# Bursts of three key tiles, casts on ScalarE and a one-pass transpose in an attention and Fourier mixing kernel

## Chip, core and metric

The kernel runs on one core of one Trainium2 chip. The metric is the device time of one execution in microseconds.

## What is computed

`x` is 2048 x 640, in fp32. The output mixes an attention block and a Fourier block by a gate for each row:

```python
qkv = x @ wqkv                       # 32 heads of 20
p = softmax(q @ k.T * 20 ** -0.5)    # for each head, 2048 x 2048
a = (p @ v) @ wo
y = Cr @ (x @ Er.T) - Ci @ (x @ Ei.T)    # DFT matrices over 640 (E) and 2048 (C)
g = sigmoid((x * gate_w).sum(-1))
out = g * a + (1 - g) * y
```

## The kernel before

One loop feeds TensorE with three kinds of work, in an order that is written out by hand.

**Scores.** Heads are taken in pairs; a unit is one pair and one half of the 1024-row halves of the queries, 32 units in all, of 32 steps each. Scores are computed twice. For the maxima, a step makes two matmuls (one for each head, on the upper and the lower 64 rows of the array, 60 of them used) at L187, and VectorE reduces each 128x512 result at L189. For the exponentials, a step makes two matmuls with 62 rows at L907 (the two more rows bring in the maximum of each query) and ScalarE takes each result through Exp at L909. Maxima run 41 steps ahead (`LEAD`). A step pair (`e` or `m`) uses one half of the array for each head; the letters' heads are set by the tuples beside the order string.

**Products with v (bursts).** The exponentials p are multiplied by v in `av_step`, L528, 21 output columns for each of two heads and two query halves: four matmuls side by side in four column groups of the array, in fp32, each of two passes. In the trace a key tile is 8 instructions. They accumulate over 16 key tiles in the bank `av`, which ScalarE copies to `o` when the unit ends (`unit_end`, L536). These matmuls stand together in a burst (`burst`), at the end of each cycle of four steps: two key tiles, 16 instructions in the trace.

**Fills.** Between the scores stand pieces of other products, split into two halves of 64 rows (banks yp0 and yp1, 320 columns): first the DFT over 640 (`hid_tile`, L363, the hidden part), then that over 2048 (`dft_step`, L608, the sequence part), then the product with `wo` (`out_tile`, L715, the output part). The sequence part has 7 products of 8 units with 16 steps of 3 fills each. `fill` issues as many as the table `goals` allows up to each letter F.

**The order.** `ORDERS` holds strings: e and m are score matmuls, F a place for fills, B the burst. The hidden part has its own string for a cycle of four steps, the sequence part another, the output part a third. A sequence unit spans three cycles.

**Operands of the sequence part.** A c part (128x1024) comes from `load_c`: one or two DMAs, a sum or difference on POOL if there are two (L501), a cast to fp32r and the difference to the cast (`split`, L114 and L115), all on POOL. Each serves 8 of a unit's 16 steps. An a tile (128x320) comes from `load_a` in the same way (L512, L517, L114, L115), and `run_extras` issues one of them in each burst while the product's turn lasts. When a unit of the sequence part ends, ScalarE and VectorE read its banks (L627, L628) and POOL adds the result to y (L742, `finish_y`).

**Maxima.** When a unit's maxima are done, `max_nm` (L203) reduces them to 128x16, `max_chain` transposes them on TensorE (L221) behind the burst, VectorE splits the result into two fp32r parts (L114, L115), and SP sends four rows into the query stack (L229, L230), before the exponentials of that unit start.

**Banks.** Five PSUM banks ps0 to ps4 rotate over the scores and transposes, one is `av`, two are yp0 and yp1. Each engine runs its instructions in the order written; SP issues all DMAs of the loop in order.

Of the kernel before, what the change touches and what calls it, by code (L numbers as in the profile page):

```python
# [18 lines left out]
P = 128  # L19
# [56 lines left out]
def mix_kernel(ctx: ExitStack, tc: tile.TileContext, xa, wqk, wb, cdft, wo, out):  # L76
# [12 lines left out]
    ps_a = pools(name="ps_a", bufs=1, space=PSUM)  # L89
# [110 lines left out]

    def max_nm(n):
        nms[n] = small.tile([P, 16], F32, name="nm", bufs=2)
        dve.tensor_reduce(nms[n], mx.pop(n).rearrange("p h q c -> p (h q) c"), axis=AX.X, op=ALU.max, negate=True)  # L203
# [14 lines left out]
    def max_chain(n):  # L218
        q = q_unit(n)
        pt = bank()[:16, :P]  # L220
        pe.transpose(pt, nms.pop(n), ident)  # L221
        m1 = small.tile([16, P], R, name="m1")
        m2 = small.tile([16, P], R, name="m2")
        split(m1, m2, pt, dve, dve)

        def rows():
            for h in range(2):
                b = 64 * h + KROWS
                sp.dma_start(f32(q[b : b + 1, :]), f32(m1[8 * h : 8 * h + 8, :]))  # L229
                sp.dma_start(f32(q[b + 1 : b + 2, :]), f32(m2[8 * h : 8 * h + 8, :]))  # L230

        if now[0] < 0:
            rows()
        else:
            at_step(now[0] + 2, rows)
# [4 lines left out]
    av = ps_a.tile([P, 512], F32, name="av")  # L240
    dve.memset(av, 0.0)
# [5 lines left out]
    def load_v(n):  # L247
# [5 lines left out]
        sp.dma_start(vts[n], v_scr[p])  # L253
# [10 lines left out]
    def load_first():  # L264
        wr, w = raw_tile()[:, : ND * P].rearrange("p (d c) -> p d c", d=ND), part_tile()
        w = w.rearrange("p z c -> p (z c)")[:, : 2 * ND * P].rearrange("p (z d c) -> p z d c", z=2, d=ND)
# [11 lines left out]
        split(w[:, 0, :1], w[:, 1, :1], wr[:, :1], act, dve)  # L278
        for d in range(ND):
            if d == 1:  # L280
                split(w[:, 0, 1:], w[:, 1, 1:], wr[:, 1:], act, dve)
            split(xs[0][:, 0, d], xs[0][:, 1, d], xr[d][1], act, dve)

    def load_wqk(c):
# [3 lines left out]
        def finish():  # L288
            w = part_tile().rearrange("p z c -> p (z c)")[:, : 2 * ND * P].rearrange("p (z d c) -> p z d c", z=2, d=ND)
            split(w[:, 0], w[:, 1], raw, act, dve)  # L290
# [26 lines left out]
    def qk_tile(c, t):  # L317
        w = wt[c]
        ps = bank()
        for d in range(ND):  # L320
            three(ps, w[:, 0, d], w[:, 1, d], xs[t][:, 0, d], xs[t][:, 1, d], d == 0, d == ND - 1)
# [13 lines left out]
    def v_pair(hf, s):  # L335
        vst = v_tile().rearrange("p s e -> p (s e)").rearrange("p (a k e) -> p a k e", a=NP // 2, k=2)
# [151 lines left out]
    def load_c(g):  # L488
# [9 lines left out]
        def finish():  # L498
            c = cparts[g] = part_tile()
            if len(raws) > 1:  # L500
                pool.tensor_tensor(raws[0], raws[0], raws[1], op=ALU.add if PRODUCTS[n][0][1][0] > 0 else ALU.subtract)  # L501
            split(c[:, 0], c[:, 1], raws[0], pool, pool)

        return finish

    def load_a(n, s):
# [7 lines left out]
        def finish():  # L514
            a = a_tile(n % 2, s)
            if len(raws) > 1:
                pool.tensor_tensor(raws[0], raws[0], raws[1], op=ALU.add if PRODUCTS[n][1][1][0] > 0 else ALU.subtract)  # L517
            split(a[:, 0], a[:, 1], raws[0], pool, pool)

        return finish  # L520

    def av_step(i, n, kt):
        v = vts[n]
        pp = [pts.pop((n, kt, qc)) for qc in range(2)]
        for qc in range(2):
            for h in range(2):
                j = 2 * qc + h
                pe.matmul(av[32 * j : 32 * j + DH + 1, :], v[:, kt, h * (DH + 1) : (h + 1) * (DH + 1)],  # L528
# [4 lines left out]
    def unit_end(i, n):  # L533
        p, u = VISITS[n]
        o = pa.tile([P, 512], F32, name="o", bufs=2)
        act.activation(o, av, AF.Copy)  # L536
# [513 lines left out]
```

## Time and profile before

| | us |
|---|---|
| median of 3 runs | 1869.67 |
| lowest and highest | 1867.93, 1871.03 |
| profiled execution | 1869.47 |
| its span | 1867.7 |
| granted clock of TensorE in it | 0.998 |

The profile's page gives, for each engine, the time in which it had an instruction running; PE is TensorE's matmuls, PEld its weight loads, DVE is VectorE, ACT ScalarE, POOL GpSimd and SP the engine that issues the DMAs. The views used below are the busy times in windows of the span, the waits (who waited for whom), the groups of instructions by line and shape, and the timeline, where instructions of one line that follow each other are merged (x16) and the first two columns are start and length. The groups give busy time and the mean length of one instruction, and idle time before them.

### The profile page before, as it was taken

Reading aid. Unit: us, or ns where it says so; the run is one execution under the profiler, and the core shown is the slowest. Engines: PE = TensorE matmul, PEld = TensorE weight load, DVE = VectorE, ACT = ScalarE, POOL = GpSimd, SP = SyncE. Lnnn points to the kernel's source line nnn. Section 1 sums busy time; section 2 is a strip of 40 time slices with the busy share of each in tenths; the row PEclk is TensorE's granted clock in tenths of the full one; section 3 lists DMA queues with packets and bytes.
Section 4 is the critical chain, followed back from the end, with each engine's and each line's share of the span. In section 5 each row is a group of like instructions: output and inputs, shape, how many; then the busy total and the mean of one; then the engine's idle time right before and its main releaser. Section 6 shows DMA issues by size and latency. Waiting matters only on the chain.

```text
span 1867.7 us, 45004 instructions
## 1 busy us (share of the span) xinstructions
PE 1858.3 (100%) x17606; PEld 1360.8 (73%) x17606; DVE 1383.7 (74%) x2310; ACT 1272.1 (68%) x2439; POOL 1162.6 (62%) x1038
## 2 busy tenths in 40 slices
PE   9999999999999999999999999999999999999998
PEld 8988777676767777777777777767777777776666
DVE  3044458787878888888888888888888888888853
ACT  4222258787877777777777777777777777778885
POOL 3335432121146897466799899867779989635544
PEclk9999999999999999999999999999999999999999
DMA  6744341222134674535567576546476766431233
GB/s 230 174 136 151 139 127 56 78 65 68 54 99 139 209 209 142 161 128 175 185 192 241 163 249 191 176 140 179 145 240 203 214 198 202 142 90 47 88 98 108
DMA packets 178771, 281.61 MB, mean 151 GB/s; under 512 B 44811, under 2 KB 113547, under 8 KB 178559
## 3 DMA queue, kind: packets, MB, share of 16 engines
q1 hardware_dynamic: 177599, 276.77, 47.4%
q0 software_dynamic: 960, 1.97, 0.6%
q8 instruction: 138, 2.26, 0.5%
q14 instruction: 74, 0.61, 0.1%
HBM read 214.61 MB, written 63.52 MB: 149 GB/s over the span
## 4 chain that ended last, share of the span: by engine, by line
PE 98%; DMA 1%; POOL 0%; ACT 0%; DVE 0%; issue 0%; SPq 0%; POOLq 0%; ACTq 0%
PE av L528 25%; PE yp L608 19%; PE ps L907 16%; PE ps L187 15%; PE yp L363 7%; PE ps L118 4%; PE ps L120 4%; PE ps L119 4%; PE yp L715 3%; PE ps L221 0%; DMA p<-in_xa 0%; POOL p L115 0%; DMA a_scr<-raw 0%; DVE mx L189 0%; ACT p L323 0%
## 5 line engine op out<-in xcount | busy, mean ns | idle before, releaser
L189 DVE TENSOR_REDUCE mx<-ps 128x1 f32<-128x512 f32 x2048 | 1280.1, 684 | 298.9 <-PE ps L187 280.7
L909 ACT ACTIVATE p<-ps 128x512 f32<-128x512 f32 x2048 | 1109.1, 599 | 371.6 <-PE ps L187 248.9
L187 PE MATMUL ps<-kst,qst 60*128 60x512 f32 x1920 | 758.3, 410 | 0.0
L907 PE MATMUL ps<-qst,kst 62*128 62x512 f32 x1920 | 744.9, 407 | 0.1
L608 PE MATMUL yp<-x,part 64*128 64x320 f32 x5376 | 662.1, 306 | 0.3 <-ACT raw L373 0.3
L608 PEld LDWEIGHTS yp<-x,part 64*128 64x128 f32 x5376 | 624.7, 186 | 8.3 <-ACT raw L373 0.6
L528 PE MATMUL av<-p,v 128*21 128x512 f32 x4096 | 490.1, 596 | 0.0
L907 PEld LDWEIGHTS ps<-qst,kst 62*128 62x128 f32 x1920 | 348.1, 185 | 182.5 <-DVE mx L189 132.2
L187 PEld LDWEIGHTS ps<-kst,qst 60*128 60x128 f32 x1920 | 342.2, 184 | 7.9 <-issue 4.2
L115 POOL TENSOR_TENSOR part<-raw,part 128x1024 fp32r<-128x1024 f32 (+1 forms) x128 | 288.0, 2250 | 10.3
L528 PEld LDWEIGHTS av<-p,v 128*21 128x21 f32 x4096 | 97.6, 100 | 221.5 <-issue 218.3
L363 PE MATMUL yp<-wb,x 64*128 64x320 f32 x1920 | 224.0, 307 | 0.0
L374 POOL TENSOR_TENSOR raw<-raw 128x320 f32<-128x320 f32 x64 | 55.7, 870 | 268.4 <-ACT raw L373 219.1
L363 PEld LDWEIGHTS yp<-wb,x 64*128 64x128 f32 x1920 | 210.1, 186 | 6.0
L114 POOL CAST part<-raw 128x1024 fp32r<-128x1024 f32 (+1 forms) x128 | 126.1, 985 | 127.9 <-PE ps L187 67.0
L501 POOL TENSOR_TENSOR raw<-raw,raw 128x1024 f32<-128x1024 f32 x77 | 185.9, 2414 | 7.5 <-DMA raw<-in_cdft 6.0
L115 POOL TENSOR_TENSOR x<-araw,x 128x320 fp32r<-128x320 f32 x112 | 97.8, 873 | 9.0
L715 PE MATMUL yp<-x,part 64*128 64x320 f32 x768 | 102.2, 308 | 0.0
L323 ACT ACTIVATE p<-ps 128x512 f32<-128x512 f32 x40 | 23.8, 597 | 102.0 <-PE ps L120 85.5
L715 PEld LDWEIGHTS yp<-x,part 64*128 64x128 f32 x768 | 92.0, 186 | 1.0
L118 PE MATMUL ps<-x,part 128*128 128x512 f32 x200 | 80.7, 403 | 1.6 <-ACT x L112 1.3
L114 POOL CAST p<-p 128x512 fp32r<-128x512 f32 x40 | 24.7, 618 | 92.4 <-ACT p L323 92.4
(110 smaller groups left out, 1419.5 us busy)
## 6 DMA issues: line engine op xcount, KB each, us to landing
raw<-in_cdft SPq DMA_DIRECT2D x192, 512.0 KB
araw<-a_scr SPq DMA_DIRECT2D x192, 160.0 KB
qk_scr<-p SPq DMA_DIRECT2D x40, 512.0 KB
kst<-qk_scr SPq DMA_DIRECT2D x84, 160.0 KB
qst<-qk_scr SPq DMA_DIRECT2D x84, 160.0 KB
yt<-y_scr SPq DMA_DIRECT2D x80, 160.0 KB
a_scr<-raw SPq DMA_DIRECT2D x64, 160.0 KB
y_scr<-yt SPq DMA_DIRECT2D x64, 160.0 KB
```

Of the source, the lines that this page charges most:

```text
L114: e1.tensor_copy(dst1, src)
L115: e2.tensor_tensor(dst2, src, f32(dst1), op=ALU.subtract)
L118: pe.matmul(ps, st1, mv1, start=first, stop=False)
L187: pe.matmul(ps, q[b : b + KROWS, qt * P : (qt + 1) * P], k[b : b + KROWS, kc * 512 : (kc + 1) * 512], start=True, stop=True)
L189: return lambda: dve.tensor_reduce(mx[n][:, h, qt, kc : kc + 1], ps, axis=AX.X, op=ALU.max)
L363: pe.matmul(yp[h][:, :HE], x[r, xz, d, cs], w[r, wz, d, :HE], start=d == 0 and z == 0, stop=d == ND - 1 and z == 2)
L501: pool.tensor_tensor(raws[0], raws[0], raws[1], op=ALU.add if PRODUCTS[n][0][1][0] > 0 else ALU.subtract)
L528: pe.matmul(av[32 * j : 32 * j + DH + 1, :], v[:, kt, h * (DH + 1) : (h + 1) * (DH + 1)], pp[qc][:, h, :], start=kt == 0, stop=kt == NS - 1)
L608: pe.matmul(yp[h][:, :HE], c[r, cz, cs], a[r, az], start=s == 0 and z == 0, stop=s == NS - 1 and z == 2)
L715: pe.matmul(yp[h][:, :HE], o[oz][r], wos[d, hf][r, wz], start=d == 0 and z == 0, stop=end)
L907: pe.matmul(pt, k[b : b + KROWS + 2, kt * P : (kt + 1) * P], q[b : b + KROWS + 2, qc * 512 : (qc + 1) * 512], start=True, stop=True)
L909: act.activation(pts[n, kt, qc][:, h], pt, AF.Exp, scale=float(DH) ** -0.5)
```

## The change

The sequence part gets a string of its own with six steps a cycle, so that a unit of it spans two cycles and a burst takes three key tiles. Since 16 key tiles aren't a multiple of three, a burst may now end one unit of scores and begin the next; the accumulator then changes banks (`next_av`) within the six that scores and accumulator share, and five are left for the scores as before. v is padded so that 32 columns instead of 21 are taken for each head. The casts of c parts and of a tiles go to ScalarE within the burst (`run_preps`), while POOL makes the sum of a c part in the fill of step 2 of 8, and the sum of an a tile one burst before its cast. Loads of a tiles are spread over the product, one a burst and two in every fourth. The buffers for parts go from 3 to 2, those for p from 5 to 7. `finish_y` comes 3 instead of 5 steps after the read at the earliest. The maxima are split into two fp32r parts before the transpose, which becomes one ordinary fp32r matmul of 128 columns of weights with the identity; a copy of its first 32 rows takes the place of the split behind it. The hidden and the output part keep their strings.

```diff
 ORDERS = (
     ("ememFFFeFFmeFFmFeFmFeFmFmFFeFemB", (0, 0, 1, 0), (1, 1, 0, 1)),
+    ("ememeFFFFmeFFemFeFmFemFeFeFmeFFmeFFFFmmemmB", (0, 0, 0, 1, 0, 1), (1, 1, 0, 1, 0, 0)),
+    ("emFeFmFeFFmFeFFmeFFmeFFmFmFeFmeB", (1, 0, 1, 1), (0, 1, 0, 0)),
     ("emFFeFmFeFFmFeFmFeFFmeFmFFmFemeB", (0, 1, 1, 0), (1, 0, 0, 1)),
-    ("emFeFmFeFFmFeFFmeFFmeFFmFmFeFmeB", (1, 0, 1, 1), (0, 1, 0, 0)),
 )
...
-    turn = itertools.count()
+    places = collections.deque(f"ps{k}" for k in range(6))
...
     def bank():
-        return ps_w.tile([P, 512], F32, name=f"ps{next(turn) % 5}")
+        places.rotate(-1)
+        return place_tile(places[-1])

     def pair_tile():
-        return work.tile([P, 2, 512], F32, name="p", bufs=5)
+        return work.tile([P, 2, 512], F32, name="p", bufs=7)
...
     def part_tile():
-        return work.tile([P, 2, 1024], R, name="part", bufs=3)
+        return work.tile([P, 2, 1024], R, name="part", bufs=2)
...
     def v_tile():
-        return work.tile([P, NS, VW], F32, name="v", bufs=2)
+        return work.tile([P, NS * VW + 16], F32, name="v", bufs=2)
...
     def max_nm(n):
-        nms[n] = small.tile([P, 16], F32, name="nm", bufs=2)
-        dve.tensor_reduce(nms[n], mx.pop(n).rearrange("p h q c -> p (h q) c"), axis=AX.X, op=ALU.max, negate=True)
+        nm = small.tile([P, 16], F32, name="nm", bufs=2)
+        dve.tensor_reduce(nm, mx.pop(n).rearrange("p h q c -> p (h q) c"), axis=AX.X, op=ALU.max, negate=True)
+        nms[n] = turned
+        split(nms[n][:, :16], nms[n][:, 16:32], nm, dve, dve)
...
-        pt = bank()[:16, :P]
-        pe.transpose(pt, nms.pop(n), ident)
-        m1 = small.tile([16, P], R, name="m1")
-        m2 = small.tile([16, P], R, name="m2")
-        split(m1, m2, pt, dve, dve)
+        pt = bank()[:, :P]
+        pe.matmul(pt, nms.pop(n), ident_r, start=True, stop=True)
+        mt = small.tile([32, P], F32, name="m1")
+        dve.tensor_copy(mt, pt[:32])
...
+    def next_av():
+        places.append(av["name"])
+        av["name"] = places.popleft()
+        av["tile"] = place_tile(av["name"])
...
-        def finish():
-            c = cparts[g] = part_tile()
+        def combine():
             if len(raws) > 1:
                 pool.tensor_tensor(raws[0], raws[0], raws[1], op=ALU.add if PRODUCTS[n][0][1][0] > 0 else ALU.subtract)
-            split(c[:, 0], c[:, 1], raws[0], pool, pool)
-
-        return finish
+
+        def parts(e1):
+            c = cparts[g] = part_tile()
+            split(c[:, 0], c[:, 1], raws[0], e1, pool)
+
+        return combine, parts
...
-    def av_step(i, n, kt):
+    def av_step(i, n, kt, split_unit):
         v = vts[n]
+        if split_unit:
+            next_av()
+        t, c0 = av["tile"], kt * VW
...
-                pe.matmul(av[32 * j : 32 * j + DH + 1, :], v[:, kt, h * (DH + 1) : (h + 1) * (DH + 1)],
+                pe.matmul(t[32 * j : 32 * j + 32, :], v[:, c0 + h * (DH + 1) : c0 + h * (DH + 1) + 32],
                           pp[qc][:, h, :], start=kt == 0, stop=kt == NS - 1)
...
-        if s % 8 == 4 and cfin and g // 8 + 2 < 2 * UNITS:
-            cfin.pop(0)()
+        if s % 8 == 2 and g // 8 + 2 < 2 * UNITS:
+            cfin[0][0]()
...
-                extras.append((now[0] + 5, functools.partial(finish_y, out_, t, m, y)))
+                extras.append((now[0] + 3, functools.partial(finish_y, out_, t, m, y)))
...
+    def run_preps(c):
+        if cfin and (done - HIDS) // 24 + 1 < 2 * UNITS:
+            cfin.pop(0)[1](act)
+        while preps["combined"]:
+            preps["combined"].pop(0)[1](act)
+        while preps["loaded"]:
+            preps["combined"].append(preps["loaded"].pop(0))
+            preps["combined"][-1][0]()
+        n = c // (2 * HT) + 1
+        if n < len(PRODUCTS):
+            k = made.get(n, 0)
+            made[n] = min(NS, k + 1 + (c % 4 == 3))
+            preps["loaded"].extend(load_a(n, s) for s in range(k, made[n]))
...
     for u in range(UNITS):
-        edge.append(edge[-1] + 3)
+        edge.append(edge[-1] + 2)
...
     def burst(c):
         for n in ends:
             max_nm(n)
-        run_extras(max(done - HIDS, 0) // 3, 2)
-        for kt in (2 * c, 2 * c + 1):
-            av_step(now[0], kt // NS, kt % NS)
+        k, _, i = phase(c)
+        steps = 6 if k == 1 else 4
+        run_extras(steps - 2)
+        if k == 1:
+            run_preps(c - HID)
+        for kt in range(i // 2, (i + steps) // 2):
+            av_step(now[0], kt // NS, kt % NS, kt % NS == 0 and kt > i // 2)
         while ends:
             max_chain(ends.pop(0))
```

`load_a` is split into `combine` and `parts` in the same way as `load_c`; the first tiles and parts, in the hidden part, are still made on POOL at once (`finished`).

More of the change, by code (lines that the diff above doesn't have):

```diff
@@ L1 @@
+import collections
 import functools
@@ L807, in mix_kernel @@
             share = count * (c + 1 - c0) // (c1 - c0) - count * (c - c0) // (c1 - c0)
-            places = order_of(c)[0].count("F")
-            goals[c] = [at_goal + share * (f + 1) // places for f in range(places)]
+            fills_ = order_of(c)[0].count("F")
+            goals[c] = [at_goal + share * (f + 1) // fills_ for f in range(fills_)]
             at_goal += share
@@ L892, in score @@
         i, z = divmod(x, 2)
-        h = z ^ first[kind][(i - (LEAD if kind == "m" else 0) - 1) % 4]
+        h = z ^ first[kind][(i - (LEAD if kind == "m" else 0) - 1 - base) % len(first[kind])]
         if kind == "m":
@@ L922, in burst @@
             next_pool()
-    first = dict(zip("em", ORDERS[0][1:]))
+    base, first = 0, dict(zip("em", ORDERS[0][1:]))
     for kind in "emme":
         score(kind)
-    for c in range(total // 4):
-        first = dict(zip("em", order_of(c)[1:]))
-        for kind in order_of(c)[0]:
+    for c in range(len(goals)):
+        k, base, i = phase(c)
+        order, *heads_ = ORDERS[k]
+        first = dict(zip("em", heads_))
+        for kind in order:
             if kind == "F":
@@ L953, in take @@
             pool.tensor_tensor(y, y, m, op=ALU.add)
-    ring = itertools.cycle([(ps_w, f"ps{k}") for k in range(5)] + [(ps_a, "av"), (ps_y, "yp0"), (ps_y, "yp1")])
+    ring = itertools.cycle([(ps_w, name) for name in (*places, av["name"])] + [(ps_y, "yp0"), (ps_y, "yp1")])
     def free_bank():
@@ L991, in mix_kernel @@
     o = tail["o"]
-    on = work.tile([P, 2, 512], R, name="p", bufs=5)
+    on = work.tile([P, 2, 512], R, name="p", bufs=7)
     lr, rs = pa.tile([P, 16], F32, name="lc"), pa.tile([P, 512], F32, name="rb")
```

89 lines of the change are left out of this document (50 added, 39 removed).

## Prediction

> **What bounds the kernel now.** I read the busy line first, then the waits of PE, then one cycle of the timeline.
>
> ```profile
> PE 1858.3 (100%) x17606; PEld 1360.8 (73%) x17606; DVE 1383.7 (74%) x2310; ACT 1272.1 (68%) x2439; POOL 1162.6 (62%) x1038
> ...
> 604.00:1665.00 1061.00, 1061.00 (x10780) 763.02 (x10780) 889.52 (x1484) 767.19 (x1423) 855.42 (x684) 1.00 0.58 181
> ```
>
> The second row is the sequence part alone (columns: window, its length, then busy time of PE, PEld, DVE, ACT, POOL). PE is busy for all of it, at full clock; DVE has 84% (889.52 of 1061), POOL 81%, ACT 72%. A busy PE may still wait inside its pipeline, so I asked what it waited for:
>
> ```profile
> PE ps L401 <- POOL ident masks.py:199: 1.4, 1, 1.4
> PE ps L118 <- ACT x L112: 1.3, 1, 1.3
> PE ps L221 <- DVE nm L203: 0.4, 1, 0.4
> ```
>
> The longest waits of PE are one of 1.4 us and one of 1.3, both at the start. So nothing that other engines do ends the work; only what PE issues, and what PE loses between its own instructions, counts. One cycle of four steps shows that loss:
>
> ```profile
> 910.65 0.39 PE L187 MATMUL ps<-kst,qst 60*128 60x512 f32 x1
> 910.68 0.39 PE L907 MATMUL ps<-qst,kst 62*128 62x512 f32 x1
> 911.00 1.91 PE L528 MATMUL av<-p,v 128*21 128x512 f32 x16
> 912.85 0.50 PE L907 MATMUL ps<-qst,kst 62*128 62x512 f32 x1
> 912.85 0.50 PE L187 MATMUL ps<-kst,qst 60*128 60x512 f32 x1
> 913.18 0.60 PE L608 MATMUL yp<-x,part 64*128 64x320 f32 x5
> ...
> 917.29 1.91 PE L528 MATMUL av<-p,v 128*21 128x512 f32 x16
> ...
> L528 PE MATMUL av<-p,v 128*21 128x512 f32 x4096 | 490.1, 596 | 0.0
> ```
>
> The first column is the start. Burst to burst takes 917.29 - 911.00 = 6.29 us. The 16 instructions of a burst are four passes of four; one takes 0.596 us (last row, the page's group), so the last pass starts 1.31 after the first and a pass costs 1.31/3 = 0.437. What 512 columns cost in an undisturbed stream is seen in the projections:
>
> ```profile
> 20.48 0.39 PE L119 MATMUL ps<-x,part 128*128 128x512 f32 x1
> 20.71 0.39 PE L120 MATMUL ps<-x,part 128*128 128x512 f32 x1
> 20.94 0.39 PE L118 MATMUL ps<-x,part 128*128 128x512 f32 x1
> ```
>
> Start to start 0.23 us. So a burst loses three pieces. Into it: 911.00 - 910.68 = 0.32 in place of 0.23, 0.09. Out of it: 912.85 - 911.00 = 1.85 for 4 x 0.437 = 1.75, 0.10. From the first scores to the first products: 0.33 in place of 0.23, 0.10. Together **0.29 us for each burst**, whatever its length.
>
> **The change, part by part.** *Longer bursts.* 56 units of three cycles (168 bursts) become 56 of two (112). Scores, products and passes keep their number; two of three burst margins stay. On PE around one burst of the sequence part (ps = score banks, av = the accumulator of before) there stood:
>
> ```order
> L907 MATMUL ps0_13340<-qst0_91,kst0_89 128x512
> L187 MATMUL ps1_13343<-kst1_90,qst1_92 128x512
> L907 MATMUL ps2_13346<-qst0_91,kst0_89 128x512
> L528 MATMUL av_104<-p_13230,v_11677 21x512 x2
> L528 MATMUL av_104<-p_13254,v_11677 21x512 x2
> L528 MATMUL av_104<-p_13282,v_11677 21x512 x2
> L528 MATMUL av_104<-p_13305,v_11677 21x512 x2
> L907 MATMUL ps3_13359<-qst0_91,kst0_89 128x512
> L187 MATMUL ps4_13362<-kst1_90,qst1_92 128x512
> ```
>
> and now, where bank ps2 is the accumulator, there stands:
>
> ```order
> L197 MATMUL ps0_11780<-kst0_86,qst0_88 128x512
> L197 MATMUL ps5_11783<-kst0_86,qst0_88 128x512
> L954 MATMUL ps4_11786<-qst1_89,kst1_87 128x512
> L197 MATMUL ps3_11789<-kst0_86,qst0_88 128x512
> L197 MATMUL ps1_11792<-kst0_86,qst0_88 128x512
> L562 MATMUL ps2_11650<-p_11599,v_9971 32x512 x2
> L562 MATMUL ps2_11650<-p_11659,v_9971 32x512 x2
> L562 MATMUL ps2_11650<-p_11677,v_9971 32x512 x2
> L562 MATMUL ps2_11650<-p_11707,v_9971 32x512 x2
> L562 MATMUL ps2_11650<-p_11728,v_9971 32x512 x2
> L562 MATMUL ps2_11650<-p_11742,v_9971 32x512 x2
> L954 MATMUL ps0_11816<-qst1_89,kst1_87 128x512
> ```
>
> Six rows lie between one pair of margins instead of four, and four of the five scores ahead of them are for maxima (L197). Removed: 56 x 0.29 = **-16.2 us**. Each half of the array still gets 12 scores and 24 products a cycle, so the new order leaves no half idle by count.
>
> *Padded v.* The weights of a pass grow from 21 to 32 columns.
>
> ```profile
> L528 PEld LDWEIGHTS av<-p,v x4096: 96/101/102, 259.8 to 1848.6; 128*21 128x21 f32 x196
> ...
> L221 PEld LDWEIGHTS ps<-ident,nm x32: 87/87/88, 219.8 to 1797.7; 128*16 128x16 f32 x32
> L187 PEld LDWEIGHTS ps<-kst,qst 60*128 60x128 f32 x1920 | 342.2, 184 | 7.9 <-issue 4.2
> ```
>
> A load takes 101 ns at 21 columns, 184 at 128: 0.8 ns a column, 9 ns for eleven. Behind a running pass that is hidden; only the first load of a burst could show, in 200 bursts: 0 to 1.8 us. From 16 to 21 columns the slope is 2.8 ns, which would make 6. I take 1.8.
>
> *The transpose of the maxima* goes from 16 to 128 columns of weights, and two small operations on VectorE move ahead of it.
>
> ```profile
> 942.42 1.92 PE L528 MATMUL av<-p,v 128*21 128x512 f32 x16
> 944.26 0.28 PE L221 MATMUL ps<-ident,nm 128*16 128x128 f32 x1
> 944.47 0.50 PE L907 MATMUL ps<-qst,kst 62*128 62x512 f32 x1
> ...
> 939.90 3.69 DVE L189 TENSOR_REDUCE mx<-ps 128x1 f32<-128x512 f32 x6
> 943.51 0.21 DVE L203 TENSOR_REDUCE nm<-mx 128x16 f32<-128x64 f32 x1
> ...
> 944.58 0.28 DVE L114 CAST m<-ps 16x128 fp32r<-16x128 f32 x1 [0.31 <-PE ps L221]
> ```
>
> It follows a burst as a score would and puts off the scores by 944.47 - 944.26 = 0.21, 31 times behind a burst, 6.5 us. Before shows no such transpose in fp32r; it may cost nothing or twice that, -6.5 to +6.5; I take 0. Its start: nm ends at 943.72, 0.54 ahead of the transpose. Two steps like nm (0.21) use 0.42 of that. In the sequence part two more maxima stand among the last scores (up to 1.2 us later) while the burst is two passes (0.87) longer; that is a wait of up to 0.2 us, 21 times: 0 to 4.2 us. I take 1.
>
> [...] The trace shows only the old form. [...]
>
> *Casts to ScalarE.* Of the chain that makes the operands, each c part (128x1024) and each a tile (128x320) is cast on ACT in a burst, and POOL keeps sums and differences. Around a burst of the sequence part ACT had (L909 are the exponentials, m the read of a finished product, o the copy of a finished accumulator)
>
> ```order
> L909 ACTIVATE p_13230<-ps4_13231 128x512
> L909 ACTIVATE p_13230<-ps1_13237 128x512
> L627 ACTIVATE m_13227<-yp0_12937 128x320
> L536 ACTIVATE o_13250<-av_104 128x512
> L909 ACTIVATE p_13254<-ps2_13255 128x512
> ```
>
> and now it holds (L113 are the casts)
>
> ```order
> L956 ACTIVATE p_13847<-ps2_13871 128x512
> L661 ACTIVATE m_13863<-yp0_13599 128x320
> L113 ACTIVATE part_13886<-raw_13601 128x1024
> L113 ACTIVATE x2_13724<-araw_13564 128x320
> L956 ACTIVATE p_13916<-ps5_13917 128x512
> ```
>
> One cast of each kind moved in here from POOL; the exponentials wait behind them, and the score banks for these. The first cast in turn waits for POOL's sum. The cover is ACT's idle time in the burst:
>
> ```profile
> L627 ACT ACTIVATE m<-yp 128x320 f32<-128x320 f32 x56 | 24.8, 443 | 0.0
> L536 ACT ACTIVATE o<-av 128x512 f32<-128x512 f32 x32 | 19.2, 600 | 24.5 <-PE av L528 20.2 <-issue 2.2 <-POOL x L114 1.0
> L112 ACT ACTIVATE x<-raw 128x1024 fp32r<-128x1024 f32 x6 | 6.4, 1062 | 9.3 <-DMA raw<-in_xa 9.3
> ...
> 917.20 1.08 ACT L909 ACTIVATE p<-ps 128x512 f32<-128x512 f32 x2 [0.39 <-PE yp L608]
> 919.73 0.60 ACT L909 ACTIVATE p<-ps 128x512 f32<-128x512 f32 x1 [1.44 <-PE ps L187]
> ```
>
> ACT idles 1.44 us now. The burst is 0.87 longer, and one exponential fewer stands right before it (0.48, from 1.08 - 0.60), so 2.8 us are free. A c part takes 1.06 us (the projections' cast); an a tile is as large as m, 0.44, or 0.88 for the two of every fourth burst; a read of m takes 0.44 and a copy of o 0.60. All of it at once is 3.0, mostly it is 2.0 or less. An overrun of 0.2 is taken up by the next exponential's bank, which PE wants again only five scores later. Cost 0; with the cover gone (two bursts in a row without idle time) each us of ACT is a us of PE.
>
> *POOL* must finish the next sum before the next cast, one chain for each cycle of (3 x 6.29 - 0.29)/2 = 9.29 us.
>
> ```profile
> L115 POOL TENSOR_TENSOR part<-raw,part 128x1024 fp32r<-128x1024 f32 x112 | 267.4, 2387 | 9.0
> L501 POOL TENSOR_TENSOR raw<-raw,raw 128x1024 f32<-128x1024 f32 x77 | 185.9, 2414 | 7.5 <-DMA raw<-in_cdft 6.0 <-PE ps L187 1.5
> ...
> L115 POOL TENSOR_TENSOR x<-araw,x 128x320 fp32r<-128x320 f32 x112 | 97.8, 873 | 9.0
> L517 POOL TENSOR_TENSOR araw<-araw 128x320 f32<-128x320 f32 x80 | 69.9, 874 | 0.7 <-DMA araw<-a_scr 0.7
> L742 POOL TENSOR_TENSOR yt<-yt,m 128x320 f32<-128x320 f32 x64 | 55.3, 876 | 6.6 <-DVE m L628 6.6
> L560 POOL TENSOR_TENSOR o<-o,rb 128x512 f32<-128x512 f32 x31 | 40.0, 1289 | 40.0 <-DMA rb<-r_scr 25.0 <-DMA y_scr<-yt 8.5 <-DMA y_scr<-m 4.5
> ```
>
> Cast 1.06, difference 2.39, a tile's difference and sum 1.75 (five in four cycles: 2.2), sum of c 2.41: 8.0 us where a product adds on both sides, with 1.2 to spare. SP is moved too: the loads of a tiles are issued in bursts, and where all six buffers are in use they wait for POOL (about 5 us behind a burst: 1.06 + 2.39 + 0.87 and the start); behind them queue the four rows of the maxima. The scores that need these come at least four steps of 1.55 us later, so they are reached by at most a us or so, in few of 21 units. Cost 0. Prologue, hidden part and output part keep their cycles.
>
> **Sum.** -16.2 + 1.8 + 0 + 1 = -13.4 us, against the profiled execution's 1869.47 (0.2 below the median of 1869.67): **1856 us**. With all bounds on one side, -16.2 - 6.5 gives 1847, and -16.2 + 6 + 6.5 + 4.2 = +0.5 gives 1870.
>
> **Rivals.** *ACT's casts become the bound* (slower). In a cycle with a second a tile (two in place of 1.25: +0.44 on the average), a norm (1.29) and both y sums (1.75, of which 1.06 beside the cast), POOL's chain is 8.0 + 0.44 + 1.29 + 0.69 = 10.4 us, over 9.29. If DMAs delay POOL as well, so that it stays over 9.29 by 0.5 in the 64 cycles of the four products with both sums, every exponential stands behind a late cast: +32 - 13 = +19, 1888 us. It decides from a chain of 9.3 us on. For it: such POOL waits exist (25.0 us for rb). Against: 1.2 us of slack, and late cycles are followed by short ones.
>
> *VectorE eats the margin* (no change). Four of the last five scores before a burst are for maxima, which VectorE takes at 3.69/6 = 0.6 us each: 2.5 us, some 0.3 of it before the burst begins. The five scores behind the burst want all five banks, 6 x 0.437 + 0.10 = 2.7 us after its start. VectorE is done about 0.5 us ahead of that. If its operations lengthen beside POOL's so that this 0.5 is used up and PE waits 0.12 us at each of 112 bursts, the 13.4 us are gone: 1870 us, and from there on it decides. For it: VectorE is the busiest helper (84%). Against: the 0.5 us, and that only two of the five wait for late maxima.
>
> *Cheaper transposes*: 6.5 us less and no pad, 1847 us.
>
> **How the numbers follow.** Forecast 0.68, ACT and POOL as the bound 0.14, VectorE 0.10, cheaper transposes 0.08. The range from 1847 to 1871 holds all but the first rival and some of the edges. A measurement of this kernel can tell about 0.2% (3.7 us): faster 0.76 (forecast and cheap transposes), same 0.09, slower 0.15.
>
> **What would show it.** Right: bursts in the sequence part 9.3 us apart, of 24 instructions, still about 0.29 lost at each; PE waits near nil. The transpose puts off the scores by 0.2 us, no more. ACT's casts lie inside the burst, with no idle time before them. Wrong: waits of PE's loads for ACT at L954 after bursts; ACT waiting for POOL at L113; cycles over 9.4 us.

## The result and the profile after

The changed kernel takes **1940.17 us** (median of 4 runs, 1933.38 to 1941.61), the kernel before, run beside it, 1870.35 (4 runs, 1867.93 to 1871.20): a ratio of 1.0367 with a 95% interval of 1.0347 to 1.0387. It is 70 us slower, where 1856 was forecast and 1847 to 1871 given as the range. The profiled execution took 1941.03 us, its span is 1939.2, and TensorE's mean granted clock fell from 0.998 to 0.989.

The busy line and the window of the sequence part (the columns as before: PE, PEld, DVE, ACT, POOL):

```profile
PE 1874.3 (97%) x17606; PEld 1394.0 (72%) x17606; DVE 1435.9 (74%) x2342; ACT 1360.4 (70%) x2645; POOL 1001.5 (52%) x852
...
613.00:1738.00 1125.00, 1071.41 (x10757) 789.67 (x10753) 933.72 (x1505) 853.80 (x1624) 688.80 (x486) 0.98 0.57 171
```

PE issues the same 17606 matmuls, and in the sequence part it is no longer busy all the time: 1125 - 1071.41 = 53.6 us are idle, where there were none. The granted clock of this part is 0.98 instead of 1.00. The casts went over as planned: POOL fell from 1162.6 to 1001.5 us, ACT rose from 1272.1 to 1360.4.

What PE waits for (us in total, times, longest):

```profile
PE ps L238 <- DVE turned L116: 46.5, 24, 3.5
PE ps L197 <- DVE mx L199: 7.0, 5, 2.2
PE ps L197 <- ACT p L956: 3.2, 1, 3.2
```

One wait holds nearly all of it: the transpose of the maxima (L238) for the second of the two small steps on VectorE that now stand ahead of it (`turned`, L116). Before, no wait of PE reached 1.5 us.

By cycles, from the starts of the bursts in the trace. From the first burst of the sequence part to the first of the output part the time went from 1060.3 to 1124.0 us, +63.7:

| part | us |
|---|---|
| clean cycles: 18.86 a unit before (3 x 6.287), 18.67 after (2 x 9.335), 56 units | -10.7 |
| the cycles with a transpose: 3.09 over a clean cycle, 21 times, 64.9 in all; before 0.21 each, 4.5 | +60.4 |
| other late cycles | +15.1 |

The sum is 64.8. The last cycle, which ends in a burst of two tiles, is 2.4 us shorter than a clean one (0.25 before), and small differences of the other cycles make up the rest. The sequence part starts 6.1 us later than before and what follows it takes 1.8 longer, which with the 63.7 makes the 71.6 between the two spans (unrounded). Of the 6.1, 1.2 is a wait of the last transpose in the hidden part, 1.8 the step into the first burst of three tiles, and 0.9 is spread over the hidden part; 2.2 are there already at the first burst of all, and I can't assign them.

One transpose in detail, first POOL, then VectorE, then PE (start, length, engine, instruction, idle time ahead and its releaser):

```profile
753.34 2.36 POOL L116 TENSOR_TENSOR part<-raw,part 128x1024 fp32r<-128x1024 f32 x1 [4.07 <-ACT part L113]
755.65 0.86 POOL L116 TENSOR_TENSOR x<-araw,x 128x320 fp32r<-128x320 f32 x1
```

```profile
753.88 0.21 DVE L218 TENSOR_REDUCE nm<-mx 128x16 f32<-128x64 f32 x1
754.13 1.60 DVE L115 CAST turned<-nm 128x16 fp32r<-128x16 f32 x1
755.76 0.78 DVE L116 TENSOR_TENSOR turned<-nm,turned 128x16 fp32r<-128x16 f32 x1
756.96 0.28 DVE L240 COPY m<-ps 32x128 f32<-32x128 f32 x1 [0.42 <-PE ps L238]
```

```profile
752.73 1.90 PE L562 MATMUL ps<-p,v 128*32 128x512 f32 x16
756.60 0.33 PE L238 MATMUL ps<-ident_r,turned 128*128 128x128 f32 x1 [1.97 <-DVE turned L116]
756.85 0.49 PE L954 MATMUL ps<-qst,kst 62*128 62x512 f32 x1
```

A cast of 16 elements for each partition takes 1.60 us and the difference 0.78; VectorE shows no idle time, so a reader of the busy times takes it for work. The ends tell otherwise: POOL's difference of the c part ends at 753.34 + 2.36 = 755.70, VectorE's cast at 755.73; POOL's next instruction ends at 756.51, VectorE's difference at 756.54. Each of the two ends 0.03 us after an instruction of POOL. ACT's cast, new in this place, is what starts POOL's difference here, within the burst, half a microsecond before nm is begun. Meanwhile PE stands: the transpose waits 1.97 us and the scores wait behind it. The reduction to nm (0.21) and the copy out of PSUM (0.28) keep their length; the first of these ran while POOL's 2.36 us were under way.

The tile's own rows say how often this happens (duration in ns: minimum, median, maximum):

```profile
L115 DVE CAST turned<-nm x32: 174/1454/1920, 219.5 to 1867.0; 128x16 fp32r<-128x16 f32 x32
L116 DVE TENSOR_TENSOR turned<-nm,turned x32: 174/781/2261, 219.7 to 1867.5; 128x16 fp32r<-128x16 f32 x32
```

The least is 0.174 us, the usual 1.454 and 0.781. In all, 23 casts and 22 differences take more than 0.25 us, and each of these 45 ends 0.028 to 0.033 us after an instruction of POOL. Before, the same two steps stood behind the transpose and read PSUM. Of the kernel before, POOL at the unit's end that the prediction quotes (its cast on VectorE stands there: 0.28 us from 944.58), and VectorE's other step:

```profile
943.58 2.37 POOL L115 TENSOR_TENSOR part<-raw,part 128x1024 fp32r<-128x1024 f32 x1
```

```profile
944.89 0.28 DVE L115 TENSOR_TENSOR m<-ps,m 16x128 fp32r<-16x128 f32 x1
```

POOL's difference runs from 943.58 to 945.95, and both steps pass under it in 0.28 us each.

The wait has a second price. PE in the microseconds behind the transpose at 756.60, as busy times with the granted clock in the third column from the right:

```profile
757.00:758.00 1.00, 1.00 (x12) 0.86 (x14) 0.82 (x2) 0.56 (x2) 0.00 (x0) 1.00 0.00 0
758.00:759.00 1.00, 1.00 (x13) 1.00 (x11) 0.94 (x3) 1.00 (x3) 0.00 (x0) 0.65 0.02 4
759.00:760.00 1.00, 1.00 (x9) 1.00 (x8) 0.46 (x1) 0.61 (x2) 0.00 (x0) 0.50 0.04 7
760.00:761.00 1.00, 1.00 (x9) 1.00 (x9) 0.65 (x1) 0.91 (x2) 0.00 (x0) 0.50 0.03 5
762.00:763.00 1.00, 1.00 (x15) 1.00 (x13) 0.73 (x2) 1.00 (x3) 0.00 (x0) 1.00 0.89 348
```

For 3.41 us from 758.3 the clock is at a half, and PE issues 9 matmuls in a microsecond instead of 15 while its busy time reads 1.00. The records of the clock have 11 such stretches in the sequence part, each 3.41 us long, and 10 of them follow a transpose that waited. Before there are none between the first microseconds and the last.

The starts of these stretches lie on one grid: any two are a whole multiple of 3.4133 us apart, to within 0.02 (the first, at 758.303, and the last, at 1656.009, by 263 of them). Which waits are followed by one seems to be a matter of their place on it. Take the periods of this grid to end 0.25 us ahead of such a start, a shift fitted to this trace: in the sequence part the 11 periods in which PE idles for 1.93 us or more are the 11 that are followed by a stretch at half clock, and no other has more than 1.84. The longest wait, 3.48 us from 1664.32, falls into two periods with 1.68 and 1.80 and is followed by none. This is a fit; no run tests it.

### The profile page after: what moved, and what is told of

The parts are those of the page before. It is cut to its first block, busy times and chain, and to the rows that moved or that the text cites. A ratio compares the mean times of both kernels' runs of the same rounds, so it can differ in the third digit from the quotient of the medians.

```text
span 1939.2 us, 44761 instructions
## 1 busy us (share of the span) xinstructions
PE 1874.3 (97%) x17606; PEld 1394.0 (72%) x17606; DVE 1435.9 (74%) x2342; ACT 1360.4 (70%) x2645; POOL 1001.5 (52%) x852
## 3 DMA queue, kind: packets, MB, share of 16 engines
q0 software_dynamic: 960, 1.97, 0.6%
q8 instruction: 138, 2.26, 0.5%
## 4 chain that ended last, share of the span: by engine, by line
PE 81%; DMA 8%; DVE 7%; SPq 1%; POOL 1%; issue 1%; ACT 0%; POOLq 0%; ACTq 0%; DVEq 0%
PE ps L562 18%; PE yp L642 15%; PE ps L954 14%; PE ps L197 12%; PE yp L385 7%; PE ps L119 4%; PE ps L120 4%; PE ps L121 4%; DVE mx L199 4%; PE yp L749 3%; DMA lc<-l_scr 2%; DVE turned L115 2%; DMA kst<-qk_scr 2%; DMA araw<-a_scr 1%; DVE turned L116 1%; DMA raw<-in_cdft 1%
## 5 line engine op out<-in xcount | busy, mean ns | idle before, releaser
L956 ACT ACTIVATE p<-ps 128x512 f32<-128x512 f32 x2048 | 1059.2, 611 | 355.6 <-PE ps L197 233.1
L954 PE MATMUL ps<-qst,kst 62*128 62x512 f32 x1920 | 736.6, 411 | 0.1
L197 PE MATMUL ps<-kst,qst 60*128 60x512 f32 x1920 | 672.9, 414 | 7.1 <-DVE mx L199 7.0
L642 PE MATMUL yp<-x,part 64*128 64x320 f32 x5376 | 644.6, 312 | 0.0
L116 POOL TENSOR_TENSOR part<-raw,part 128x1024 fp32r<-128x1024 f32 (+1 forms) x128 | 287.1, 2243 | 396.7 <-ACT part L113 376.1
L562 PE MATMUL ps<-p,v 128*32 128x512 f32 x4096 | 481.0, 597 | 0.0
L197 PEld LDWEIGHTS ps<-kst,qst 60*128 60x128 f32 x1920 | 323.1, 186 | 20.8 <-DVE mx L199 9.0
L562 PEld LDWEIGHTS ps<-p,v 128*32 128x32 f32 x4096 | 113.1, 109 | 242.2 <-issue 236.8
L113 ACT ACTIVATE part<-raw 128x1024 fp32r<-128x1024 f32 (+2 forms) x121 | 123.4, 1020 | 7.3 <-POOL raw L522 5.3
L749 PE MATMUL yp<-x,part 64*128 64x320 f32 x768 | 102.3, 309 | 0.0
L116 POOL TENSOR_TENSOR x<-araw,x 128x320 fp32r<-128x320 f32 x112 | 97.4, 877 | 1.3
L345 ACT ACTIVATE p<-ps 128x512 f32<-128x512 f32 x40 | 23.7, 597 | 104.5 <-PE ps L121 101.4
L119 PE MATMUL ps<-x,part 128*128 128x512 f32 x200 | 81.6, 408 | 1.3 <-ACT x L113 1.1
L120 PE MATMUL ps<-x,part 128*128 128x512 f32 x200 | 80.0, 400 | 0.2 <-DVE x L116 0.2
```

What stands on the lines that cost most here:

```text
L116: e2.tensor_tensor(dst2, src, f32(dst1), op=ALU.subtract)
L119: pe.matmul(ps, st1, mv1, start=first, stop=False)
L120: pe.matmul(ps, st1, mv2, start=False, stop=False)
L197: pe.matmul(ps, q[b : b + KROWS, qt * P : (qt + 1) * P], k[b : b + KROWS, kc * 512 : (kc + 1) * 512], start=True, stop=True)
L562: pe.matmul(t[32 * j : 32 * j + 32, :], v[:, c0 + h * (DH + 1) : c0 + h * (DH + 1) + 32], pp[qc][:, h, :], start=kt == 0, stop=kt == NS - 1)
L642: pe.matmul(yp[h][:, :HE], c[r, cz, cs], a[r, az], start=s == 0 and z == 0, stop=s == NS - 1 and z == 2)
```

## The experiments

My theory after this result: the loss comes from the two small steps on VectorE, which now read and write SBUF and stand still while POOL's instruction runs (A). Rivals: the new order, the long bursts or the casts on ACT cost it (B), or the transpose itself as a 128-column matmul does, without a wait (C).

**1. The change with the old path of the maxima.** Bursts, casts and loads as changed; transpose and split as before.

```diff
...
     def max_nm(n):
-        nm = small.tile([P, 16], F32, name="nm", bufs=2)
-        dve.tensor_reduce(nm, mx.pop(n)..., negate=True)
-        nms[n] = turned
-        split(nms[n][:, :16], nms[n][:, 16:32], nm, dve, dve)
+        nms[n] = small.tile([P, 16], F32, name="nm", bufs=2)
+        dve.tensor_reduce(nms[n], mx.pop(n)..., negate=True)
...
-        pt = bank()[:, :P]
-        pe.matmul(pt, nms.pop(n), ident_r, start=True, stop=True)
-        mt = small.tile([32, P], F32, name="m1")
-        dve.tensor_copy(mt, pt[:32])
+        pt = bank()[:16, :P]
+        pe.transpose(pt, nms.pop(n), ident)
+        m1 = small.tile([16, P], R, name="m1")
+        m2 = small.tile([16, P], R, name="m2")
+        split(m1, m2, pt, dve, dve)
...
```

> The changed kernel with the maxima's path of before: 128x16 transposed first, then split by VectorE from the bank. Theory A (in the changed kernel the cast and the subtraction ahead of the transpose, both from SBUF, wait on VectorE until POOL's running instruction ends, TensorE waits behind them, and a wait that long sometimes halves the clock): the transposes' excess of 64.9 us shrinks to the 4.5 it had in before, and about 1941 - 60 - 4 = 1877 us result, 1870 to 1884. Theory B (the six-step order, the long bursts or the casts on ScalarE cost it): above 1910 us. Theory C (the ordinary matmul of 128 columns costs it by itself, without a wait): about 1877 too, but then the fourth run of this set can't show TensorE filled during the wait.

Measured: 1882.94 us (6 runs, 1874.51 to 1892.17), a ratio of 1.0078 [1.0054, 1.0103]. So 57 of the 70 us go with the path of the maxima. A and C both say so, B doesn't; experiments 3 and 4 tell A from C. The profiled execution is the longest of the six, 1892.17 us, so that its waits are above the usual. What PE waits for in it:

```profile
PE ps L197 <- DVE mx L199: 12.2, 5, 5.3
...
PE ps L197 <- ACT p L950: 1.5, 1, 1.5
...
PE ps L231 <- DVE nm L213: 0.4, 1, 0.4
```

The wait of the transpose is gone, and from the start of the burst's last instruction to the transpose it is 0.523 us again (before 0.523; in the changed kernel 2.65 on the average). What is left, 13 us in the median, is of another kind: five waits of scores for VectorE's maxima, and four stretches at half clock behind such waits (mean clock 0.995). VectorE's own wait, and the longest of these:

```profile
DVE lc L578 <- DMA lc<-l_scr: 13.6, 5, 5.6
```

```profile
1196.82 1.29 DVE L199 TENSOR_REDUCE mx<-ps 128x1 f32<-128x512 f32 x2 [0.18 <-PE ps L197]
1203.70 0.25 DVE L578 RECIPROCAL lc<-lc 128x16 f32<-128x16 f32 x1 [5.59 <-DMA lc<-l_scr]
1203.87 1.22 DVE L199 TENSOR_REDUCE mx<-ps 128x1 f32<-128x512 f32 x2
```

The reciprocal of a unit's sums (0.25 us) is written into VectorE's stream at a fixed step; its operand comes by DMA, and where this is late, every maximum behind it stands. Here SP issued the load at 1195.43 and the reciprocal started 8.3 us later; the DMA engines were 86 to 92% busy from 1195 to 1202.

**2. The kernel before with the new path of the maxima alone.** The same lines the other way round, in the kernel before; two-tile bursts and POOL's casts stay.

```diff
...
+        nms[n] = turned
+        split(nms[n][:, :16], nms[n][:, 16:32], nm, dve, dve)
...
-        pt = bank()[:16, :P]
-        pe.transpose(pt, nms.pop(n), ident)
-        m1 = small.tile([16, P], R, name="m1")
-        m2 = small.tile([16, P], R, name="m2")
-        split(m1, m2, pt, dve, dve)
+        pt = bank()[:, :P]
+        pe.matmul(pt, nms.pop(n), ident_r, start=True, stop=True)
+        mt = small.tile([32, P], F32, name="m1")
+        dve.tensor_copy(mt, pt[:32])
...
```

> The kernel before with the maxima's new path alone: split from SBUF ahead of an ordinary matmul. Theory A: POOL is busy 81% of the sequence part here, so most of the 21 transposes there wait: some 1.5 to 2.5 us each, with half-clock windows 1890 to 1925 us. Theory B: no change, within 3 us of 1870. The rival that only the shorter time between the last maximum and the transpose in the six-step cycles matters: also near 1870, as nm here ends 0.5 us ahead of the transpose and two steps need 0.42.

Measured: 1905.65 us (4 runs, 1904.89 to 1906.80), 1.0199 [1.0182, 1.0216]: this part alone loses 36 us without longer bursts and without a cast on ACT. The wait, and the casts of three units that follow each other:

```profile
PE ps L228 <- DVE turned L115: 24.5, 18, 2.5
```

```profile
698.01 1.97 DVE L114 CAST turned<-nm 128x16 fp32r<-128x16 f32 x1
...
752.47 0.17 DVE L114 CAST turned<-nm 128x16 fp32r<-128x16 f32 x1
...
803.07 2.06 DVE L114 CAST turned<-nm 128x16 fp32r<-128x16 f32 x1
```

At 698.01 POOL was in a difference of a c part that ended at 699.95, and the cast ended at 699.98. At 752.47 the cast met no such instruction and took 0.17. Here the phase of POOL against the burst varies: of the 21 cycles with a transpose in the sequence part, 15 are 0.4 us or more over a clean one. In the change, where ACT's cast starts POOL's difference in the burst, it is 20.

**3. The change with POOL's difference in four pieces.** If VectorE waits for the end of the instruction of POOL that is running, shorter instructions make shorter waits, at the same work for POOL.

```diff
-            split(c[:, 0], c[:, 1], raws[0], e1, pool)
+            act.activation(c[:, 0], raws[0], AF.Copy) if e1 is act else e1.tensor_copy(c[:, 0], raws[0])
+            for q in range(0, 1024, 256):
+                pool.tensor_tensor(c[:, 1, q : q + 256], raws[0][:, q : q + 256], f32(c[:, 0, q : q + 256]), op=ALU.subtract)
```

> The changed kernel with POOL's subtraction for a c part in four pieces of 256 columns. Theory A: the cast ahead of the transpose ends when a piece ends, after 0.6 us or less in place of 1.6 us, and the subtraction after one more piece; the step from the burst to the transpose falls from 2.65 to 1.0 to 1.8 us, and the time to 1890 to 1925 us. A rival, that the two operations are slow for a reason of their own: 2.65 us and 1941 stay.

Measured, in one run: 1901.84 us, 38 less than the change. The tile of the maxima:

```profile
L115 DVE CAST turned<-nm x32: 174/506/5422, 219.0 to 1827.8; 128x16 fp32r<-128x16 f32 x32
L116 DVE TENSOR_TENSOR turned<-nm,turned x32: 174/647/651, 219.2 to 1828.3; 128x16 fp32r<-128x16 f32 x32
```

The cast's median fell from 1454 to 506 ns and the difference's maximum from 2261 to 651, which is about one piece of POOL's (four take 2.78 us). The step from the burst to the transpose fell from 2.65 to 1.52 us, and the stretches at half clock from 11 to 3 (mean clock 0.989 and 0.997). This separates the two readings of VectorE's long instructions: the work on VectorE is the same, only POOL's instructions are shorter. The one cast of 5.42 us shows that the end of an instruction of POOL doesn't always let VectorE in. POOL, then VectorE:

```profile
1366.38 2.78 POOL L528 TENSOR_TENSOR part<-raw,part 128x256 fp32r<-128x256 f32 x4
1369.11 0.86 POOL L116 TENSOR_TENSOR x<-araw,x 128x320 fp32r<-128x320 f32 x1
1369.93 2.34 POOL L522 TENSOR_TENSOR raw<-raw,raw 128x1024 f32<-128x1024 f32 x1
```

```profile
1366.88 5.42 DVE L115 CAST turned<-nm 128x16 fp32r<-128x16 f32 x1
1372.33 0.18 DVE L116 TENSOR_TENSOR turned<-nm,turned 128x16 fp32r<-128x16 f32 x1
```

POOL ran six instructions with no gap, and the cast came through when the last one ended, at 1369.93 + 2.34 = 1372.27; its own end is 1372.30.

**4. The change with PE kept busy during the wait.** Nine matmuls that nobody reads (their bank is written again by the transpose, so the output stays) stand ahead of each transpose from the sequence part on.

```diff
         pt = bank()[:, :P]
+        for _ in range(9 if now[0] >= 224 else 0):
+            pe.matmul(pt, ident, ident, start=True, stop=True)
         pe.matmul(pt, nms.pop(n), ident_r, start=True, stop=True)
```

> The changed kernel with nine fp32 matmuls of 128 columns (identity by identity, results overwritten) ahead of each transpose from the sequence part on, some 1.9 us of TensorE work in the time in which it waits. Theory A: the waits stay (burst to transpose 2.5 to 3 us) but no half-clock window follows them: about 17 us less, 1920 to 1928 us. If the half clock has another cause: still about ten windows and 1938 to 1950 us.

Measured, in one run: 1935.13 us, where 1920 to 1928 was expected. The total misses, the mechanism holds. At the transposes:

```profile
645.94 2.27 PE L239 MATMUL ps<-ident 128*128 128x128 f32 x18
648.32 0.33 PE L240 MATMUL ps<-ident_r,turned 128*128 128x128 f32 x1
```

The start of the transpose comes no earlier, but no stretch at half clock follows one any more (three are left, behind other waits; mean clock 0.996). The cycles with a transpose cost 51.7 us over clean ones instead of 64.9: 13 us of the loss were the clock, or 15 with the 2.0 that the nine matmuls add at the one transpose that had not waited. The total, 1935.13, lies within the change's own four times (1933.38 to 1941.61) and shows nothing by itself. Of the two profiled executions it is 5.9 us shorter, 7 less than those 13: 4.9 went in the output part, where the nine matmuls stand ahead of three transposes that had waited little or not at all (2.55 us behind the burst each, in the change 1.09, 1.12 and 0.52), and the rest in small differences before the sequence part and in its other cycles.

**5. Experiment 1 with the reciprocal later.** The steps at which a unit's sums are inverted and used move back, so that the load has six steps more.

```diff
-        steps = (6, 10, 16, 23, 27, 34, 45) if n < NU - 4 else (1, 4, 7, 8, 11, 14, 16)
+        steps = (6, 10, 22, 26, 30, 38, 47) if n < NU - 4 else (1, 4, 7, 8, 11, 14, 16)
```

> The second run's kernel e1 (changed, with the old path of the maxima), in which the reciprocal of the sums is issued 22 steps after a unit's end instead of 16, and what follows it later in step. Theory D (what is left of the loss: loads of the sums lc come late behind SP's waits for a tiles' buffers, VectorE's reciprocal waits for them in its queue, and the maxima and TensorE behind it): the 13.6 us in which VectorE waits for lc vanish, and the half-clock windows behind them; 1859 to 1866 us, below before. Theory E (the rest is the order, the banks or ScalarE's casts): 1878 to 1888 as in e1.

Measured: 1871.26 us (11 runs, 1868.94 to 1875.72), 1.0009 [1.0001, 1.0018]. That is 11.7 less than experiment 1; VectorE waits for no load of lc, and the clock is full from the first stretch to the last (mean 0.999). But 1859 to 1866 was expected, and the time is that of the kernel before to 0.1%, not less. What PE's matmuls wait for:

```profile
PE ps L119 <- ACT x L113: 2.6, 1, 2.6
...
PE ps L197 <- ACT p L950: 1.2, 1, 1.2
```

The first is at the start of the kernel. So no wait of PE's matmuls explains why longer bursts bring nothing. The sequence part itself is shorter, 1056.5 us for 1060.3. Against the kernel before, in the profiled executions: clean cycles -10.7, cycles with a transpose +6.0 (0.50 each instead of 0.21), one late cycle +1.6, small differences of the others +1.4, the step from the hidden part into the first burst of three tiles +1.4, the last cycle with its burst of two tiles -2.2, hidden and output part +0.8 each, ahead of the first burst +0.4; together -0.5. The trace of experiment 1 shows where the 0.3 us at a transpose go, PE and then VectorE:

```profile
643.94 0.28 PE L231 MATMUL ps<-ident,nm 128*16 128x128 f32 x1
...
644.49 0.91 PE L948 MATMUL ps<-qst,kst 62*128 62x512 f32 x2
644.90 1.08 PE L636 MATMUL yp<-x,part 64*128 64x320 f32 x9
```

```profile
644.25 0.28 DVE L115 CAST m<-ps 16x128 fp32r<-16x128 f32 x1 [0.37 <-PE ps L231]
644.56 0.28 DVE L116 TENSOR_TENSOR m<-ps,m 16x128 fp32r<-16x128 f32 x1
```

Behind a burst the new order has five scores ahead of the first fills, and the transpose has taken one of the five banks. The fifth score gets this bank only when VectorE has read it twice, at 644.56 + 0.28 = 644.84; the fills at 644.90 follow it. The waits of PE's weight loads name it, here in experiment 5, once for each of the 21 transposes of the sequence part:

```profile
PEld ps L948 <- DVE m L116: 9.6, 21, 0.5
```

The kernel before has no such wait.

**6. Experiment 5 with the casts back on POOL.**

```diff
-            cfin.pop(0)[1](act)
+            cfin.pop(0)[1](pool)
         while preps["combined"]:
-            preps["combined"].pop(0)[1](act)
+            preps["combined"].pop(0)[1](pool)
```

> e5_late_recip with the casts back on POOL instead of ScalarE, each at the same place in the program. If the casts on ScalarE cost or bring nothing by themselves (ScalarE idles over 1 us at each burst): within 4 us of e5. If POOL's longer chain then delays the parts: 5 to 30 us above e5, with TensorE waiting for POOL at the products. If ScalarE's casts hold back exponentials in e5: below e5.

Measured: 1871.66 us (10 runs, 1867.74 to 1876.94), 1.0013 [1.0002, 1.0023], 0.4 from experiment 5. The casts on ACT neither cost nor bring anything once the maxima don't pay for POOL's instructions.

**7 and 8. More buffers for a tiles.** SP waits for the buffers of a tiles far more than before (rows of 32.3 and 15.5 us then; this one is that of the change):

```profile
SPq L541 <- POOL x L116: 200.0, 46, 8.4
```

If these waits delay the load of lc, two buffers more for each second term should free SP. This went into experiment 1 (7) and experiment 5 (8).

```diff
-            raws.append(apool[0].tile([P, HE], F32, name="araw", bufs=6))
+            second = raws and len(apool) > 1
+            raws.append(apool[1].tile([P, HE], F32, name="arawb", bufs=2) if second else apool[0].tile([P, HE], F32, name="araw", bufs=6))
```

> e1 with two more buffers for the second terms of a tiles, so that SP waits less for them, and the reciprocal at step 16 as in e1. Theory D: SP's waits for those buffers fall from 172 us to below 70, VectorE's waits for lc from 13.6 to below 6, and the time by 6 to 15 us against e1, to 1868 to 1877. If lc is late because of the traffic on the DMA engines alone: waits for lc and time as in e1 (1883).

> e5_late_recip with those two more buffers as well. Theory D: as e5 or up to 3 us less, 1857 to 1866 us, since with the late reciprocal nothing on VectorE waits for SP any more.

Measured: 1893.53 us (4 runs, 1881.54 to 1895.80), 1.0117 [1.0089, 1.0144], and 1871.80 us (11 runs, 1868.74 to 1876.65), 1.0018 [1.0009, 1.0027]. Both miss; 7 is 10.6 us slower than experiment 1, and VectorE's waits for lc are 16.4 us in its trace instead of 13.6. The edit didn't do what it was made for, as SP's row of experiment 7 shows:

```profile
SPq L536 <- POOL araw L540: 195.8, 39, 8.8
```

The wait moved to the two new buffers, which stay in use until POOL has made the sum. So these runs say nothing on whether SP's queue delays the load of lc. What can be said is that with later reciprocals (8) the two buffers change nothing, and that VectorE waits for no load of lc there either.

## Why the prediction was wrong

**The step that failed** is the one on the transpose of the maxima: "Two steps like nm (0.21) use 0.42 of that", and from it a wait of 0 to 4.2 us, of which I took 1. The two steps use 2.2 us at their medians and the wait in the sequence part is 21 x (2.65 - 0.523) = 44.7 us, to which the clock adds 13 to 15 (experiment 4). I took the price from nm, an instruction of VectorE alike in size, and asked only when the step could start, not what else must be over before it can end. The rows that I quoted gave no price for it: the steps that were removed had read PSUM, and nm, though it reads SBUF, passes under POOL's instructions (in the changed kernel 23 of its 32 lie whole within one, and all take 0.21 to 0.22 us). The trace of the kernel before did hold the case, outside the loop: VectorE's subtraction of `wb` (128x966, both operands in SBUF) took 2.15 us at 19.23 and at 117.90, where a subtraction of POOL's was running, and 1.17 at 66.29 and at 97.42. I had bounded the cost from an undisturbed row only. Experiments 1 and 2 show that this part makes the loss, 57 us with and 36 us without the rest of the change, and experiment 3 that it is POOL's instruction which VectorE waits for.

**The transpose itself.** I took 0, between -6.5 and +6.5. The score behind it starts 756.85 - 756.60 = 0.25 us later, before 0.21: 31 x 0.04 is 1.2 us. Right. Its start by itself is hardly later: where the last transpose of the sequence part didn't wait, it came 0.538 us behind the burst's last instruction, against 0.523 for the old form.

**Longer bursts.** I took -16.2, with the pad -14.4; the clean cycles bring -10.7. A clean cycle was to be (3 x 6.287 - 0.29)/2 = 9.29, and it is 9.335:

```profile
723.79 2.78 PE L562 MATMUL ps<-p,v 128*32 128x512 f32 x24
726.50 0.50 PE L954 MATMUL ps<-qst,kst 62*128 62x512 f32 x1
...
733.11 1.48 PE L562 MATMUL ps<-p,v 128*32 128x512 f32 x10
```

The margins are as forecast: from the burst's last instruction to the first score 0.523 us before and after, from the last score to the burst 0.32. The burst of six passes is as long as six passes are. What is longer is the stretch between, from the first score behind a burst to the last one ahead of the next: 6.30 us. Before it is 4.122; with the last score's own 0.23, less the 0.10 that the prediction counts as lost at the first scores, this is 4.25 for four steps, so 6.38 for six, and without that 0.13 again 6.25. About 0.05 us a cycle are lost, 112 times. I had said that the order leaves no half of the array idle by count; by time it seems to, but this is argued from the trace. No experiment puts the same counts in another order.

**The pad of v.** 1.8 us forecast: in the bursts of two tiles, which the hidden and the output part keep, the first instruction to the last goes from 1.322 to 1.332 us, 0.010 for each burst. Right, if small.

**Casts on ACT, and POOL.** 0 forecast for both; experiment 6 finds 0.4 us. PE's only wait for the exponentials is the one of 3.2 us, at 1653 us, where ACT's cast had waited 5.3 us for a sum of POOL's and this for a load; the rival of 1888 us by ACT and POOL as the bound didn't come. But ACT's cast sets when POOL's difference starts, and so puts it under the maxima in nearly every cycle with a transpose. That this turns the 36 us of experiment 2 into the 57 here is argued; no run has the new path and long bursts with the casts on POOL.

**SP and VectorE.** Loads on SP were put down as nothing. In the changed kernel three late cycles of 2.3 to 2.6 us, in experiment 1 waits of 13.6 us, come from a load of lc that lands late and a reciprocal that holds VectorE. The step failed in that I followed the rows of the maxima behind SP, not the load of lc. Both SP's queue and the DMA engines seem to make it late: in the sequence part of the kernel before, SP issued each such load at least 7.7 us ahead of its reciprocal. Of the three that make late cycles in the changed kernel, two let VectorE go on 4.2 and 4.1 us after SP issued them (at 690.7 and 1011.1), so SP was late with them; the third took 9.4 us from the issue (at 1222.1), and the longest wait of experiment 1 8.3. No run separates the two causes. The rival "VectorE eats the margin" named the right engine with the wrong mechanism: not its load, but what its instructions wait for.

**After the repair.** Without the maxima's new path and with later reciprocals the change should have been 1859 to 1866 by its own terms. It stays at 1871: the order of scores and fills leaves 10.7 us of the 14.4, and small terms eat these, the transpose's bank (6.0) first, then single late cycles and small differences (3.0) and the hidden and output part (1.6, of which the pad of v, 0.010 at each of 88 bursts, makes 0.9). No version beats the kernel before.

## What to carry to other kernels

Before a small step is moved ahead of an instruction that the busiest engine waits for, look at where its operands lie and at which long instruction of another engine runs at that moment; here a step of 0.17 us lasted up to 2.26, and once, in experiment 3, 5.42. A long "busy" time of a tiny instruction can be a wait: compare its end with the ends on the other engines. And when a few tenths of a microsecond are saved at each of many places, list beforehand what each place needs next (a bank, a load, a half of the array), since each of those can take the tenths back without a wait of a matmul; read the waits of the weight loads too.

## What the runs showed of the hardware

- A 128x16 cast from SBUF to SBUF on VectorE takes 0.174 us when POOL doesn't hold it up, and otherwise ends 0.03 us after an instruction of POOL that was running; so does a subtraction with two operands in SBUF. Where POOL's instructions follow each other without a gap, it can wait for the last of six (5.42 us); elsewhere it came in between two, as at 755.73 in the changed kernel. A reduction from SBUF (0.21) and steps that read PSUM (0.28) run on under the same instruction of POOL.
- Of the 20 transposes of the sequence part that waited (1.95 to 2.40 us, one 3.48), 10 were followed by 3.41 us at half clock, and not the one of 3.48. The starts of such stretches lie on a grid of 3.4133 us. With matmuls in the wait none followed a transpose.
- A stretch at half clock doesn't show in PE's busy time, which reads 1.00 in it; only the granted clock and the count of matmuls (9 for 15) do.
